# The head mix ahead of the softmax in one float32 matmul, and a new column order for the mixed weights

## The chip, the cores and the metric

The kernel runs on one core of a Trainium2 chip. The metric is the device time of one execution in microseconds, taken over three runs. The core has TensorE (PE, matmuls; PEld is its weight load), VectorE (DVE), ScalarE (ACT), GpSimd (POOL), and SyncE (SP), which issues the transfers.

## The reference

Attention over 2 batches, 12 heads, 448 positions, 64 features a head, in which the heads are mixed before and after the softmax; then two expert layers on the 896 rows of 768 features. All is float32, and the experts' weights come as float64.

```python
scores = scale * np.matmul(q, k.transpose(0, 1, 3, 2))
scores = np.einsum('bhij,hg->bgij', scores, w_pre)
scores = scores - np.max(scores, axis=-1, keepdims=True)
attn = np.exp(scores)
attn = attn / (np.sum(attn, axis=-1, keepdims=True) + 1e-09)
attn = np.einsum('bhij,hg->bgij', attn, w_post)
x = np.matmul(attn, v)          # then heads side by side: 896 x 768
h = x @ w_in                    # first experts: 768 -> 2048 -> 768
x = (h * np.clip(h + 3.0, 0.0, 6.0) / 6.0) @ w_out
h = x @ w_in2                   # second experts
out = (np.maximum(h, 0.0) + alpha * np.minimum(h, 0.0)) @ w_out2
```

## The kernel before

The 448 query rows of a batch are cut into tiles of 120, 120, 120 and 88 rows, eight tiles in all. A tile's scores are made head by head (`qk`): keys and queries are split into two float32r parts (`split_k`, `split_q`), two matmuls give 120 x 448 scores in PSUM, and a copy, mostly on ACT, puts them into S, which holds rows on the partitions and heads side by side.

To mix heads, a matmul needs the heads on the partitions. So a tile is cut into groups of ten rows with all their 12 heads, 120 partitions. Group o of a tile takes the rows o, o + 12, o + 24 and so on (o, o + 8, ... in the tile of 88 rows, whose last 8 rows are a group of their own): 45 groups a batch, 90 in all. `pull` regroups them by a transfer from S. `round_s` rounds the group to float32r (shi, on DVE or, for the first tile, on POOL), and `split_and_norm` takes the remainder (slo, on DVE). `premix` then multiplies by the mixing weights, which lie ten times on the diagonal of a 120 x 120 matrix: high weights times shi, low weights times shi, high weights times slo, three float32r matmuls into one place in PSUM (mx); DVE takes the rows' maximum (nm). `exp` is the softmax's exponential on ACT, with the row sums (sm). One step later `split_and_norm` turns the sums over and multiplies the second mixing matrix by them (wr, on DVE). Three steps later (LAG) `post` mixes with wr, in plain float32, four matmuls with the four key blocks of e as the stationary operand; its result (pt) has keys on the partitions and row x of head g at column 12 x + g. `post_evac` copies it on ACT into MT, where a head's rows lie in their order in the tile: its elements land 12 (or 8) elements and 120 elements apart. `av` multiplies MT by the values for pairs of heads, float32 again, and the result is copied to xT by DVE, or for the last two tiles split at once into two float32r parts by `split_x` (ACT and DVE).

Everything is emitted by hand in one loop over steps, and every engine takes its instructions in that order. Step s issues the regrouping of group s + 4 (PL), then premix(s), the scores due in this step for the next tile (0 to 3 heads), exp(s), the copies of the scores, loads and splits of queries (and, for the first tile of the second batch, of keys), the remainder of group s + 2 with the sums of group s - 1, post(s - 3) with its copy, the value product due for the tile before (every second step or so), and what the experts need early. SP issues all transfers in one queue, in the same order; the regrouping has four buffers, each free again when slo is made. After the loop come the last tile's value products and the experts: products of three float32r matmuls each, with the weights converted beside them by ACT, DVE and POOL.

Of the kernel before, what the change touches and what calls it, by code (L numbers as in the profile page):

```python
# [7 lines left out]
F32 = mybir.dt.float32  # L8
R = mybir.dt.float32r
# [4 lines left out]
ALU = mybir.AluOpType  # L14
# [3 lines left out]
LAG = 3  # steps from a group's premix to its mix after the softmax  # L18
HI = "VVAVVAVVAVVA"  # which engine rounds each head's first keys
PL = 4  # steps from the regrouping of a group's rows to their premix  # L20
EB = 384  # output features of an out-layer that are worked on together
# The high words of 2**-127 and of the largest float32, read as float32.
# [4 lines left out]
def spread(items, lo, hi):  # L27
    """items over the steps lo..hi-1, evenly and in order."""
    out = {}
    n = max(1, hi - lo)  # L30
    for i, it in enumerate(items):
        out.setdefault(lo + i * n // len(items), []).append(it)
    return out
# [3 lines left out]
def kernel(  # L37
    ctx: ExitStack,
    tc: tile.TileContext,
    q: bass.AP,  # [B, 2 D, per query tile: H, rows], the D rows twice  # L40
    k0: bass.AP,  # first batch: [2 D, H / 2, S], the D rows of two heads
    k: bass.AP,  # the others: [B - 1, 2 D, H, S], the D rows twice
    v: bass.AP,  # [B, 112, H, 4, D]: key 112 * t + p at [p, :, t]
    w_pre: bass.AP,  # the 12 x 12 block 10 times on the diagonal
    w_post: bass.AP,
    w_in1: bass.AP,  # int64 words of float64, [block, 128, 768]
# [4 lines left out]
    out: bass.AP,  # transposed  # L51
):
    nc = tc.nc
# [32 lines left out]
    # Pools that end early lie on top of their side, so that what follows lands there.  # L86
# [13 lines left out]
    with tc.manual_schedule():  # L100
# [4 lines left out]
        # ---------------------------------------------------------------- attention  # L105
# [8 lines left out]
        def load_k0(p, z):  # L114
            # the second tile's scores come later to this place
            if p == 0:
                k_st[0] = s_odd.tile([128, H, S], F32, tag="S", name="k0")
            nc.sync.dma_start(out=k_st[0][:, p:z, :], in_=k0[:, p:z, :])
# [17 lines left out]
        # The rows of k and what float32r leaves of them: [hi; lo], or [lo; hi] for the  # L136
        # odd heads of the first batch, which lie on the upper partitions.
# [42 lines left out]
        d_t, hi_t, hl_t, mx_t, e_t, sm_t, wr_t, pt_t = {}, {}, {}, {}, {}, {}, {}, {}  # L180

        def pull(g):
            ti, o, st, xn = groups[g]
            t = late.tile([GP, S], F32, tag="pull", bufs=4, name="pull")
            src = S_t[ti][bass.ds(o, xn, step=st)] if st > 1 else S_t[ti][o:o + xn]
            nc.sync.dma_start(t[:xn * H], src)
            d_t[g] = t

        def round_s(g, eng):
            pn = groups[g][3] * H  # L190
            hi = late.tile([GP, S], R, tag="shi", bufs=3, name="shi")
            eng.tensor_scalar(hi[:pn], d_t[g][:pn], 1.0, 1.0, ALU.mult, ALU.mult)  # L192
            hi_t[g] = hi

        # The rows of group g are split while the row sums of group gn are turned over.
        def split_and_norm(g, gn):
            if gn in sm_t:
                pm = groups[gn][3] * H
                sm = sm_t.pop(gn)[:pm]
                nc.vector.tensor_scalar(sm, sm, 1e-9, None, ALU.add)  # L200
            if g < NG:
                pn = groups[g][3] * H
                if g not in hi_t:
                    round_s(g, nc.vector)
                d, hi = d_t.pop(g)[:pn], hi_t.pop(g)
                lo = late.tile([GP, S], R, tag="slo", bufs=2, name="slo")
                hl_t[g] = (hi, lo)
            if gn in e_t:
                nc.vector.reciprocal(sm, sm)
            if g < NG:  # L210
                nc.vector.tensor_tensor(lo[:pn], d, hi[:pn].bitcast(F32), ALU.subtract)  # L211
            if gn in e_t:
                wr = wr_t[gn] = late.tile([GP, GP], F32, tag="wr", bufs=LAG + 1, name="wr")
                nc.vector.tensor_scalar(wr[:pm, :pm], wpost[:pm, :pm], sm, None, ALU.mult)  # L214

        def premix(g):
            pn = groups[g][3] * H
            hi, lo = hl_t.pop(g)
            m = psA.tile([GP, 512], F32, tag="mx", bufs=2, name="mx")
            nc.tensor.matmul(m[:pn, :S], wph[:pn, :pn], hi[:pn], start=True, stop=False)  # L220
            nc.tensor.matmul(m[:pn, :S], wpl[:pn, :pn], hi[:pn], start=False, stop=False)  # L221
            nc.tensor.matmul(m[:pn, :S], wph[:pn, :pn], lo[:pn], start=False, stop=True)  # L222
            nm = late.tile([GP, 1], F32, tag="nm", name="nm")
            nc.vector.tensor_reduce(nm[:pn], m[:pn, :S], axis=AX.X, op=ALU.max, negate=True)  # L224
            mx_t[g] = (m, nm)
# [11 lines left out]
        def post(g):  # L237
            pn = groups[g][3] * H
            e, wr = e_t.pop(g), wr_t.pop(g)
            p = psA.tile([JP, 512], F32, tag="pt", bufs=2, name="pt")  # L240
            for c in range(NJ):
                nc.tensor.matmul(  # L242
                    p[:, c * pn:(c + 1) * pn], e[:pn, c * JP:(c + 1) * JP], wr[:pn, :pn],
                    start=True, stop=True,
                )
            pt_t[g] = p

        def post_evac(g):
            ti, o, st, xn = groups[g]
            pn = xn * H  # L250
            if ti not in MT:
                MT[ti] = late.tile([JP, NJ, H, GP], F32, tag="MT", bufs=2, name="MT")
            p = pt_t.pop(g)
            dst = MT[ti][:, :, :, o:o + (xn - 1) * st + 1:st].rearrange("p t g x -> p t x g")
            nc.scalar.copy(dst, p[:, :NJ * pn].rearrange("p (t x g) -> p t x g", t=NJ, g=H))  # L255
# [3 lines left out]
        def av(ti, a):  # L259
# [12 lines left out]
            if a % 3 == 2:  # L272
                if ti >= NTILE - 2:
                    for z in range(3):
                        split_x(a - 2 + z, 1, T["i0"], T["i0"] + n, p[:, z, :n], nc.vector)
                else:
                    c0 = T["b"] * S + T["i0"]
                    nc.vector.tensor_copy(xT[:, a - 2:a + 1, c0:c0 + n], p[:, :, :n])

        # which head of which tile is worked on at which step  # L280
# [12 lines left out]
        # ---------------------------------------------------------------- experts  # L293
# [7 lines left out]
        NE = 2  # feature tiles whose results for the first batch have a place of their own  # L301
        NC = 3  # feature tiles whose products for the first batch go ahead
# [16 lines left out]
        # float64 words to float32, rounded to nearest: the exponent's bias changes by  # L319
        # dropping three bits, and the 29 low bits are rounded into the mantissa. What  # L320
        # float32 can't hold becomes zero or its largest number.
# [80 lines left out]
        def split_x(kk, c, a, z, src, eng):  # L402
            if (kk, c) not in x_t:
                x_t[kk, c] = pair(P[f"x{c}"], "x")
            h, l = x_t[kk, c]
            nc.scalar.copy(h[:, a:z], src)
            eng.tensor_tensor(l[:, a:z], src, h[:, a:z].bitcast(F32), ALU.subtract)
# [19 lines left out]
        # An activation in two parts, between which its engines take other work.  # L427
# [54 lines left out]
        # ---------------------------------------------------------------- attention, emitted  # L482
# [8 lines left out]
        for nm, src in (("pre", w_pre), ("post", w_post)):  # L491
            wmix[nm] = (kq if nm == "pre" else late).tile(
                [GP, GP], F32, tag=f"wmix_{nm}", bufs=1, name=f"wmix_{nm}"
            )
# [15 lines left out]
        wpre, wpost = wmix["pre"], wmix["post"]  # L510
        wph = late.tile([GP, GP], R, tag="wph", bufs=1, name="wph")
        wpl = late.tile([GP, GP], R, tag="wpl", bufs=1, name="wpl")
        nc.gpsimd.tensor_scalar(wpre, wpre, scale, 1.0, ALU.mult, ALU.mult)
        nc.gpsimd.tensor_scalar(wph, wpre, 1.0, 1.0, ALU.mult, ALU.mult)
        nc.gpsimd.tensor_tensor(wpl, wpre, wph.bitcast(F32), ALU.subtract)
# [9 lines left out]
        # the experts' first loads and splits, beside the last tile's groups  # L525
# [26 lines left out]
        for s_ in range(-PL, NG + LAG):  # L552
# [36 lines left out]
            if 1 <= s_ + 3 < tiles[1]["s"]:  # L589
                round_s(s_ + 3, nc.gpsimd)  # L590
            if s_ >= -2:
                split_and_norm(s_ + 2, s_ - 1)
# [25 lines left out]
        # ---------------------------------------------------------------- experts, emitted  # L618
# [65 lines left out]
def _laid_out(q, k, v, w_pre, w_post, moe_w_in, moe_w_out, moe2_w_in, moe2_w_out, moe2_alpha):  # L684
    """The inputs' elements in the order in which the kernel reads them."""
# [66 lines left out]
```

## Time and profile before

| | us |
|---|---|
| median of 3 runs | 744.57 |
| lowest, highest | 742.71, 744.76 |
| profiled execution: span from first to last instruction | 740.6 |
| PE busy in it | 707.6 |
| DVE busy | 503.5 |
| ACT busy | 414.9 |
| POOL busy | 345.6 |

The page gives the profiled execution's time as its span; what lies around the span is in the runs' times alone, 4.0 us by the median. The attention takes about the first 273 us of the span, the experts the rest. The busy time of PE is a union of overlapping matmuls, each counted until its last result is out, so it is more than what the matmuls cost one after the other.

### The profile page before, as it was taken

The page shows a single profiled execution, that of the slowest core. Times are in us where ns is not written, and L with a number is a line of the kernel's source. Part 1 is how long each engine was busy: PE and PEld are TensorE (multiplying, and loading weights), DVE is VectorE, ACT ScalarE, POOL GpSimd, SP SyncE. Part 2 cuts the span into 40 slices and gives each one's busy share as a digit, 9 for nine tenths or more (in the row PEclk, how much of TensorE's full clock was granted, in tenths as well). Part 3 has the DMA queues.
Part 4 walks back from the last instruction along what each step waited for, and adds up shares of the span by engine and source line. Part 5 has one row for each costly group of instructions (what it writes and reads, how often), then busy time and mean ns, then how long its engine had stood idle before and what let it go on. Part 6 is the DMA issues. An engine that isn't in the chain of part 4 may idle for free.

```text
span 740.6 us, 11533 instructions
## 1 busy us (share of the span) xinstructions
PE 707.6 (96%) x4254; PEld 627.0 (85%) x4254; DVE 503.5 (68%) x964; ACT 414.9 (56%) x699; POOL 345.6 (47%) x230
## 2 busy tenths in 40 slices
PE   5899978999998999999999999999999999999998
PEld 3678866898876889888889999999999999999997
DVE  7898899888989837777776344346777778435311
ACT  4688866888887745666654354334544444333310
POOL 4341166221315314565657856453555555654530
PEclk9999999999999999999999999999999999999999
DMA  4643454336435202323233432322333332424302
GB/s 150 202 150 111 161 168 96 126 123 215 151 104 101 87 2 92 121 87 127 87 104 128 152 129 90 123 90 82 90 123 101 114 114 103 160 93 161 128 1 74
DMA packets 31621, 85.60 MB, mean 116 GB/s; under 512 B 5198, under 2 KB 21710, under 8 KB 31566
## 3 DMA queue, kind: packets, MB, share of 16 engines
q1 hardware_dynamic: 31566, 84.87, 34.7%
q8 instruction: 34, 0.56, 0.3%
q14 instruction: 21, 0.17, 0.1%
HBM read 62.84 MB, written 2.75 MB: 89 GB/s over the span
## 4 chain that ended last, share of the span: by engine, by line
PE 63%; DVE 18%; issue 9%; POOL 6%; DMA 2%; ACT 2%; SPq 0%; POOLq 0%; DVEq 0%; ACTq 0%
PE p L411 49%; DVE slo L211 5%; PE pt L242 4%; POOL wb L349 4%; PE av L268 4%; DVE nm L224 3%; DVE shi L192 3%; DVE wr L214 2%; PE sc L175 2%; PE mx L220 2%; DMA pull<-S 2%; POOL wlo L360 1%; PE mx L221 1%; PE mx L222 1%; DVE kT L153 1%
## 5 line engine op out<-in xcount | busy, mean ns | idle before, releaser
L360 POOL TENSOR_TENSOR wlo<-wb,whi 128x768 fp32r<-128x768 f32 x64 | 133.0, 2079 | 166.9 <-ACT whi L354 164.4
L349 POOL TENSOR_TENSOR wb<-wb,wst 128x768 int32<-128x768 int32 x64 | 130.5, 2039 | 66.3 <-DVE wb L342 39.4
L411 PE MATMUL p<-xh,wlo 128*128 128x448 f32 x384 | 141.4, 368 | 2.0 <-POOL wlo L360 1.4
L411 PE MATMUL p<-gh,wlo 128*128 128x448 f32 x384 | 141.2, 368 | 0.1
L411 PE MATMUL p<-gh,whi 128*128 128x448 f32 x384 | 141.0, 367 | 0.0
L411 PE MATMUL p<-gl,whi 128*128 128x448 f32 x384 | 141.0, 367 | 0.0
L411 PE MATMUL p<-xh,whi 128*128 128x448 f32 x384 | 140.6, 366 | 0.0
L411 PE MATMUL p<-xl,whi 128*128 128x448 f32 x384 | 140.3, 365 | 0.0
L334 DVE TENSOR_SCALAR wb<-wb 128x768 f32<-128x768 f32 x64 | 64.2, 1003 | 97.0 <-ACT wb L326 96.9
L326 ACT ACTIVATE wb<-wst 128x768 f32<-128x768 f32 x64 | 58.3, 911 | 74.1 <-DMA wst<-in_w_out_dram 43.6
L255 ACT COPY MT<-pt 112x480 f32<-112x480 f32 (+1 forms) x90 | 96.4, 1071 | 1.9 <-PE pt L242 1.9
L242 PEld LDWEIGHTS pt<-wr,e 120*112 120x112 f32 x720 | 85.6, 176 | 9.7 <-ACT MT L255 3.7
L242 PE MATMUL pt<-wr,e 120*112 120x120 f32 x720 | 89.7, 267 | 1.2 <-DVE wr L214 0.7
L232 ACT ACTIVATE e<-mx,nm 120x448 f32<-120x448 f32 (+1 forms) x90 | 57.3, 637 | 49.4 <-DVE sm L200 33.8
L411 PEld LDWEIGHTS p<-xh,wlo 128*128 128x128 f32 x384 | 72.1, 188 | 11.7 <-POOL wlo L360 6.2
L354 ACT CAST whi<-wb 128x768 fp32r<-128x768 f32 x64 | 53.2, 832 | 47.3 <-PE p L411 44.9
L411 PEld LDWEIGHTS p<-gh,wlo 128*128 128x128 f32 x384 | 72.2, 188 | 7.4 <-POOL wlo L360 0.8
L411 PEld LDWEIGHTS p<-gh,whi 128*128 128x128 f32 x384 | 72.2, 188 | 6.5
L411 PEld LDWEIGHTS p<-gl,whi 128*128 128x128 f32 x384 | 72.2, 188 | 6.4
L411 PEld LDWEIGHTS p<-xl,whi 128*128 128x128 f32 x384 | 72.2, 188 | 5.6
L411 PEld LDWEIGHTS p<-xh,whi 128*128 128x128 f32 x384 | 72.1, 188 | 5.6
L175 PE MATMUL sc<-kT,qT 128*120 128x448 f32 (+1 forms) x192 | 58.4, 397 | 15.8 <-DVE kT L153 7.5
(60 smaller groups left out, 1046.5 us busy)
## 6 DMA issues: line engine op xcount, KB each, us to landing
wst<-in_w_in_dram SPq DMA_DIRECT2D x32, 768.0 KB
wst<-in_w_out_dram SPq DMA_DIRECT2D x32, 768.0 KB
pull<-S SPq DMA_DIRECT2D x88, 210.0 KB
qst<-in_q_dram SPq DMA_DIRECT2D x24, 180.0 KB
v<-in_v_dram SPq DMA_DIRECT2D x8, 336.0 KB
kst<-in_k_dram SPq DMA_DIRECT2D x4, 672.0 KB
out_dram<-o SPq DMA_DIRECT2D x12, 224.0 KB
qst<-in_q_dram SPq DMA_DIRECT2D x8, 132.0 KB
```

The lines of the kernel that those rows point to most:

```text
L175: nc.tensor.matmul(p[:n, :S], t[:, o, a:a + n], kT[h], start=(o == 0), stop=(o == 1))
L211: nc.vector.tensor_tensor(lo[:pn], d, hi[:pn].bitcast(F32), ALU.subtract)
L232: nc.scalar.activation(out=e[:pn], in_=m[:pn, :S], func=ACTF.Exp, bias=nm[:pn], accum_out=sm[:pn])
L242: nc.tensor.matmul(p[:, c * pn:(c + 1) * pn], e[:pn, c * JP:(c + 1) * JP], wr[:pn, :pn], start=True, stop=True,)
L255: nc.scalar.copy(dst, p[:, :NJ * pn].rearrange("p (t x g) -> p t x g", t=NJ, g=H))
L268: nc.tensor.matmul(p[64 * o:64 * o + 64, a % 3, :n], v_t[T["b"], h // HC][:, h % HC, c, :], MT[ti][:, c, h, :n], start=(c == 0), stop=(c = ...
L326: nc.scalar.activation(t, s[:, :, 1].bitcast(F32), ACTF.Abs)
L334: nc.vector.tensor_scalar(t, t, W_MAX, W_MIN, ALU.min, ALU.max)
L349: nc.gpsimd.tensor_tensor(n, n, st_t.pop(i)[:, :, 0].bitcast(I32), ALU.add)
L354: nc.scalar.copy(hi, b_t[i])
L360: nc.gpsimd.tensor_tensor(lo, b_t.pop(i), w_t[i][0].bitcast(F32), ALU.subtract)
L411: nc.tensor.matmul(p, wt[a], xt[c], start=(first and z == 0), stop=(last and z == 2))
```

## The change

- `premix` is one float32 matmul on the regrouped rows as they came. `round_s`, the remainder, and the high and low parts of the first mixing matrix are gone.
- The regrouping has PL + 2 = 6 buffers, each free when its premix is done.
- `split_and_norm` becomes `norm`, the turning over of the sums alone.
- The columns of the second mixing matrix are put into another order once, on POOL, so that `post` gives row x of head g at column 10 g + x. `post` always takes all 120 columns.
- MT holds a tile's rows in the order of the groups, so that `post_evac` writes runs of ten elements.
- The rows come back into order behind the value products: `by_row` gives the copy to xT, and the split of the last two tiles, a reading pattern with every tenth row next to each other; a tile of 88 rows is copied in two pieces, 80 and 8 rows.
- Comments are removed, and the first mixing matrix lies in another pool.

```diff
         def pull(g):
-            t = late.tile([GP, S], F32, tag="pull", bufs=4, name="pull")
+            t = late.tile([GP, S], F32, tag="pull", bufs=PL + 2, name="pull")
...
-        def round_s(g, eng):
-            pn = groups[g][3] * H
-            hi = late.tile([GP, S], R, tag="shi", bufs=3, name="shi")
-            eng.tensor_scalar(hi[:pn], d_t[g][:pn], 1.0, 1.0, ALU.mult, ALU.mult)
-            hi_t[g] = hi
...
+        def norm(g):
+            pm = groups[g][3] * H
+            sm = sm_t.pop(g)[:pm]
+            nc.vector.tensor_scalar(sm, sm, 1e-9, None, ALU.add)
+            nc.vector.reciprocal(sm, sm)
+            wr = wr_t[g] = late.tile([GP, GP], F32, tag="wr", bufs=LAG + 1, name="wr")
+            nc.vector.tensor_scalar(wr[:pm], wpost[:pm], sm, None, ALU.mult)
...
         def premix(g):
             pn = groups[g][3] * H
-            hi, lo = hl_t.pop(g)
+            d = d_t.pop(g)
             m = psA.tile([GP, 512], F32, tag="mx", bufs=2, name="mx")
-            nc.tensor.matmul(m[:pn, :S], wph[:pn, :pn], hi[:pn], start=True, stop=False)
-            nc.tensor.matmul(m[:pn, :S], wpl[:pn, :pn], hi[:pn], start=False, stop=False)
-            nc.tensor.matmul(m[:pn, :S], wph[:pn, :pn], lo[:pn], start=False, stop=True)
+            nc.tensor.matmul(m[:pn, :S], wpre[:pn, :pn], d[:pn], start=True, stop=True)
...
-                    p[:, c * pn:(c + 1) * pn], e[:pn, c * JP:(c + 1) * JP], wr[:pn, :pn],
+                    p[:, c * GP:(c + 1) * GP], e[:pn, c * JP:(c + 1) * JP], wr[:pn],
...
-            p = pt_t.pop(g)
-            dst = MT[ti][:, :, :, o:o + (xn - 1) * st + 1:st].rearrange("p t g x -> p t x g")
-            nc.scalar.copy(dst, p[:, :NJ * pn].rearrange("p (t x g) -> p t x g", t=NJ, g=H))
+            p = pt_t.pop(g)[:, :NJ * GP].rearrange("p (t g x) -> p t g x", t=NJ, g=H)
+            r = o * G if st > 1 else o
+            nc.scalar.copy(MT[ti][:, :, :, r:r + xn], p[:, :, :, :xn])
+
+        def by_row(dst, src, n):
+            m = n // G * G
+            d, s = dst[..., :m], src[..., :m]
+            if len(dst.shape) == 3:
+                yield (d.rearrange("p z (x o) -> p z x o", x=G), s.rearrange("p z (o x) -> p z x o", x=G))
+            else:
+                yield (d.rearrange("p (x o) -> p x o", x=G), s.rearrange("p (o x) -> p x o", x=G))
+            if n > m:
+                yield dst[..., m:n], src[..., m:n]
...
-                        split_x(a - 2 + z, 1, T["i0"], T["i0"] + n, p[:, z, :n], nc.vector)
+                        h, l = x_pair(a - 2 + z, 1)
+                        for d, r, s in zip(
+                            (d for d, _ in by_row(h[:, T["i0"]:T["i0"] + n], p[:, z, :n], n)),
+                            (d for d, _ in by_row(l[:, T["i0"]:T["i0"] + n], p[:, z, :n], n)),
+                            (s for _, s in by_row(h[:, T["i0"]:T["i0"] + n], p[:, z, :n], n)),
+                        ):
+                            nc.scalar.copy(d, s)
+                            nc.vector.tensor_tensor(r, s, d.bitcast(F32), ALU.subtract)
                 else:
-                    nc.vector.tensor_copy(xT[:, a - 2:a + 1, c0:c0 + n], p[:, :, :n])
+                    for d, s in by_row(xT[:, a - 2:a + 1, c0:c0 + n], p[:, :, :n], n):
+                        nc.vector.tensor_copy(d, s)
...
+        wpost = late.tile([GP, GP], F32, tag="wpost", bufs=1, name="wpost")
+        nc.gpsimd.tensor_copy(
+            wpost.rearrange("p (g x) -> p x g", g=H), wmix["post"].rearrange("p (x g) -> p x g", g=H)
+        )
...
-        nc.gpsimd.tensor_scalar(wph, wpre, 1.0, 1.0, ALU.mult, ALU.mult)
-        nc.gpsimd.tensor_tensor(wpl, wpre, wph.bitcast(F32), ALU.subtract)
...
-            if 1 <= s_ + 3 < tiles[1]["s"]:
-                round_s(s_ + 3, nc.gpsimd)
-            if s_ >= -2:
-                split_and_norm(s_ + 2, s_ - 1)
+            if s_ - 1 in range(NG):
+                norm(s_ - 1)
```

## Rows read from the trace of the kernel before

**Rows 1.** The page's chain of work that ended last: shares of the span by engine.

```profile
PE 63%; DVE 18%; issue 9%; POOL 6%; DMA 2%; ACT 2%; SPq 0%; POOLq 0%; DVEq 0%; ACTq 0%
```

**Rows 2.** The busy table of five stretches: start and end of the stretch, its length, then for PE, PEld, DVE, ACT and POOL the busy us (and instructions), the granted clock of PE, the share of the transfer engines and their GB/s.

```profile
23.50:58.60 35.10, 30.59 (x190) 23.54 (x191) 31.14 (x85) 27.38 (x58) 14.38 (x21) 1.00 0.56 177
58.60:97.40 38.80, 38.80 (x339) 34.09 (x337) 32.78 (x95) 30.99 (x61) 7.54 (x10) 1.00 0.43 145
97.40:129.70 32.30, 25.24 (x206) 20.46 (x204) 32.30 (x73) 20.98 (x42) 20.88 (x20) 1.00 0.44 119
129.70:175.00 45.30, 45.30 (x409) 40.59 (x408) 39.16 (x118) 38.13 (x76) 10.56 (x13) 1.00 0.41 140
...
221.30:258.00 36.70, 32.20 (x274) 26.99 (x274) 34.25 (x82) 26.68 (x55) 18.00 (x13) 1.00 0.40 96
```

**Rows 3.** The timeline of PE over two steps of a PE-bound stretch: start, length from the first start to the last end, engine, line, operation, tiles, and how many instructions the row merges.

```profile
63.15 0.38 PE L268 MATMUL av<-MT,v 112*64 112x120 f32 x4
63.45 0.47 PE L220 MATMUL mx<-shi,wph 120*120 120x448 f32 x1
63.76 0.37 PE L221 MATMUL mx<-shi,wpl 120*120 120x448 f32 x1
...
64.17 0.57 PE L175 MATMUL sc<-kT,qT 128*120 128x448 f32 x2
64.58 0.98 PE L242 MATMUL pt<-wr,e 120*112 120x120 f32 x8
65.33 0.44 PE L220 MATMUL mx<-shi,wph 120*120 120x448 f32 x1
...
67.34 1.04 PE L268 MATMUL av<-MT,v 112*64 112x120 f32 x16
68.31 0.47 PE L220 MATMUL mx<-shi,wph 120*120 120x448 f32 x1
```

**Rows 4.** PE's instructions grouped by line in three stretches (23.5 to 58.6, 97.4 to 129.7, 221.3 to 258.0): how many, busy us and the mean ns of one, the idle time before them and what ended it. The last row is from PE's waits in 175.0 to 221.3: total us, times, longest.

```profile
L242 PE MATMUL pt<-wr,e 120*112 120x120 f32 x104 | 13.4, 272 | 0.1
L220 PE MATMUL mx<-shi,wph 120*120 120x448 f32 x16 | 7.0, 437 | 3.2 <-POOL shi L192 2.0 <-ACT e L232 0.8 <-POOL qT L161 0.3
L175 PE MATMUL sc<-kT,qT 128*120 128x448 f32 x22 | 6.5, 371 | 0.1
...
L242 PE MATMUL pt<-wr,e 120*112 120x120 f32 x72 | 8.9, 265 | 0.0
L175 PE MATMUL sc<-kT,qT 128*120 128x448 f32 x24 | 7.3, 383 | 7.1 <-ACT S L578 7.0
L268 PE MATMUL av<-MT,v 112*64 112x120 f32 x82 | 5.5, 272 | 0.0
...
L242 PE MATMUL pt<-wr,e 120*112 120x120 f32 x106 | 13.5, 269 | 1.0 <-DVE wr L214 0.7 <-ACT MT L255 0.2
L268 PE MATMUL av<-MT,v 112*64 112x120 f32 x112 | 7.3, 272 | 1.3 <-ACT MT L255 1.3
L220 PE MATMUL mx<-shi,wph 120*120 120x448 f32 (+1 forms) x12 | 5.4, 452 | 0.7 <-DVE sm L209 0.5 <-ACT e L232 0.2
L411 PE MATMUL p<-xh,whi 128*128 128x448 f32 x7 | 2.7, 380 | 0.0
...
PE av L268 <- ACT MT L255: 1.7, 1, 1.7
```

**Rows 5.** Groups of instructions by line and shape, whole run: count, busy us, mean ns of one, idle time before them.

```profile
L192 DVE TENSOR_SCALAR shi<-pull 120x448 fp32r<-120x448 f32 x77 | 39.5, 513 | 0.0
L211 DVE TENSOR_TENSOR slo<-pull,shi 120x448 fp32r<-120x448 f32 x88 | 69.6, 792 | 3.7 <-POOL shi L192 3.6
L255 ACT COPY MT<-pt 112x480 f32<-112x480 f32 x88 | 94.6, 1075 | 1.9 <-PE pt L242 1.9
L255 ACT COPY MT<-pt 112x384 f32<-112x384 f32 x2 | 1.8, 904 | 0.0
L578 ACT COPY S<-sc 120x448 f32<-120x448 f32 x57 | 29.8, 532 | 1.6 <-PE sc L175 1.6
```

**Rows 6.** The page's group of the mix after the softmax, the group of the value products of 88 rows, and the timeline row of the last tile's.

```profile
L242 PE MATMUL pt<-wr,e 120*112 120x120 f32 x720 | 89.7, 267 | 1.2 <-DVE wr L214 0.7
L268 PE MATMUL av<-MT,v 112*64 112x88 f32 x192 | 8.8, 243 | 0.0
268.94 3.86 PE L268 MATMUL av<-MT,v 112*64 112x88 f32 x96
```

**Rows 7.** The busy table of three early stretches, columns as in rows 2.

```profile
24.00:26.00 2.00, 1.62 (x8) 1.30 (x8) 2.00 (x4) 0.10 (x2) 1.31 (x3) 1.00 0.19 73
26.00:32.00 6.00, 5.45 (x33) 4.24 (x31) 5.83 (x18) 4.94 (x12) 1.15 (x2) 1.00 0.87 261
32.00:40.00 8.00, 5.65 (x33) 3.87 (x32) 4.32 (x15) 4.73 (x10) 2.54 (x5) 1.00 0.79 228
```

**Rows 8.** The timeline of ACT behind the last tile's value products, idle time in brackets, and from the waits of 274 to 390 us that of the experts' products for converted weights (total us, times, longest).

```profile
271.02 0.23 ACT L406 CAST xh<-av 128x88 fp32r<-128x88 f32 x1 [0.55 <-PE av L268]
271.57 0.23 ACT L406 CAST xh<-av 128x88 fp32r<-128x88 f32 x1 [0.32 <-DVE xl L407]
274.07 0.91 ACT L326 ACTIVATE wb<-wst 128x768 f32<-128x768 f32 x1
...
PEld p L411 <- POOL wlo L360: 6.6, 12, 1.8
```

## What I predicted

> **What bounds the kernel now.** I read the chain of the whole run first: 63% of it is TensorE (PE) and 18% VectorE (DVE) [rows 1]. So both matter, and the next question is where each does. The busy table by stretch answers it [rows 2]: look for stretches in which one engine has no idle time. From 58.6 to 97.4 us and from 129.7 to 175.0 PE is busy for the whole stretch. From 97.4 to 129.7 it is DVE that is busy for all 32.30 us while PE has 25.24. In 23.5 to 58.6 and 221.3 to 258.0 DVE is near full too. So the attention alternates: PE-bound stretches pay for every PE nanosecond that is added, and DVE-bound stretches pay back what DVE loses. The granted clock is 1.00, its 2.4 GHz level, in all of them.
>
> Busy time of a pipelined matmul is not its price; its price is the distance between starts. In a PE-bound step [rows 3] the premix's second pass starts at 63.76 and what follows the third at 64.17: 0.203 us each, so 0.61 for three. The 8 passes of the mix after the softmax take 0.98 with a last one of 0.265 long, so (0.98 - 0.265) / 7 = 0.102 each, 0.82 for eight. A step without the value product runs from 63.45 to 65.33, 1.88 us; one with it from 65.33 to 68.31, 2.98. The value product therefore costs 1.10.
>
> From these prices and the counts of three slow stretches [rows 4] comes the idle time that PE could get rid of:
> - 23.5 to 58.6 (the first value product ends it): 16 x 0.61 + 22 x 0.203 + 13 x 0.82 + 1 x 1.10 = 26.0 of 35.1; idle 9.1.
> - 97.4 to 129.7 (72 / 8 = 9 whole steps): 9 x 0.61 + 24 x 0.203 + 9 x 0.82 + 5 x 1.10 = 23.2 of 32.3; idle 9.1.
> - 221.3 to 258.0: 12 x 0.61 + 13.2 x 0.82 + 7 x 1.10 + 20 x 0.203 (first expert products; one of three like rows is shown) = 29.9 of 36.7; idle 6.8.
> In 175.0 to 221.3 one wait on the copy of the mixed weights counts, 1.7 [rows 4].
>
> **The change, part by part.**
>
> **DVE loses the rounding and the remainder.** Per group shi (0.513) and slo (0.792) go: 39.5 + 69.6 = 109 us of DVE, and 11 roundings of GpSimd (POOL) [rows 5]. In 97.4 to 129.7 that leaves DVE about 32.3 - 9 x 1.3 to 32.3 - 9 x 1.84 (there slo is dearer), 16 to 21 us for work that PE needs 23 for; DVE is no longer the bound. Nothing that is left of DVE's work stands in front of the premix: its input is the regrouping transfer itself, issued four steps ahead.
>
> **PE: one float32 matmul instead of three float32r ones.** The trace has no float32 matmul of 448 columns, but it has two kinds of narrow ones. The mix after the softmax shows two passes for each (720 for 90 x 4). The value products show what a column costs: 96 passes of 88 columns in 3.86 us [rows 6] are (3.86 - 0.243) / 95 = 0.0381 each, 16 of 120 columns in 1.04 [rows 3] are (1.04 - 0.266) / 15 = 0.0516. They run in pairs, one on each half of the output: four take 0.38, which is 0.266 and one distance of 0.10, not three of 0.0516 [rows 3]. So a pair, and each pass in it, is 0.076 and 0.103: 0.84 ns for each column, and next to nothing fixed. One pass of 448 columns is then 448 x 0.84 = 0.376, two are 0.752, against 0.61: +0.143 for a group, +12.9 us for 90, where PE is the bound. Bounds: if the halves of a pair were really served in turn, a column costs half and a pass no less than the 0.203 of a float32r pass of that width: 0.406, a gain of 0.203 a group (18.3 us). From above four float32r passes: 0.812, +0.203 (18.3 us). I take 0.752, since the four in 0.38 speak for passes side by side.
>
> The Trainium skill ("FP8 and Floating Point Precision", TensorE Precision Notes) says that true float32 takes four passes through the array. The trace shows two instructions for each; at 0.84 ns for a column each is worth two. By four passes at float32r's price the premix would cost the upper bound, and the sum below would lose its gain almost wholly.
>
> **Regrouping transfers.** Six buffers instead of four, freed by the premix and no longer by slo. It matters in the beginning only: from 24 to 26 us the transfers run at 73 GB/s for want of a buffer, then at 261 and 228 [rows 7]. All of 24 to 40 at 261 would be (146 + 1566 + 1824) / 261 = 13.5 us instead of 16: the first nine groups come at most 2.5 us sooner, whatever DVE does. So of the 9.1 us of the first stretch I keep 3.0.
>
> **The copy of the mixed weights (ACT).** 480 scattered elements take 1.075, 384 take 0.904: 1.78 ns each over a fixed 0.22. A dense copy of 448 takes 0.532, so (0.532 - 0.22) / 448 = 0.70 [rows 5]; runs of ten should come near 0.22 + 480 x 0.70 = 0.56; the bounds are 0.56 and 1.075. 90 x 0.5 = 46 us of ACT go, but ACT is the bound in no stretch [rows 2]: worth the 1.7 us wait above and a part of 0.8 in the first stretch. Without that cover the copy is what the value product waits for.
>
> **The turned column order** (the permuted weights once on POOL, which is busy 14.4 of 35.1 us in the first stretch [rows 2], and 120 instead of 96 columns for two groups) is nothing. The rows come back into order when the value product leaves PSUM. On DVE, which has room now, that costs nothing; for the last tile it does. Its six copies and six subtractions alternate, ACT then DVE, 0.55 a pair, and the next conversion follows at 274.07 directly [rows 8]. 88 rows become a piece of 80 and one of 8: at about 0.53 and 0.38 a pair of pieces, 0.36 more for each of six, 2.2 in all on that thread. The experts then wait for converted weights (6.6 us in 12 waits [rows 8]), so a later start of the conversions is not swallowed; but PE itself starts on the first pieces at once. I take 1.5, bounds 0 and 2.5.
>
> The Trainium skill ("Advanced Engine Details and Errata", PSUM Cachelines) has 8-byte lines in PSUM and asks for two elements in a row; the reading by every tenth element breaks that. By the scattered price of 1.78 ns against 0.70, 80 elements would take 0.09 longer in each of 12 instructions, 1.0 us more at the end; the trace has no such read.
>
> **The sum.** Idle time that goes: 6.1 in the first stretch; 7.1 in the second (POOL has 20.9 us of work there [rows 2] and would fill 24 to nine tenths, so I keep 2); 1.7; 5.8 in the last (I keep 1). Together 20.7. Against it +12.9 on PE and +1.5 at the end: -6.3. The profile's span is 740.6, the median 744.6, 4 us around the span that the change doesn't touch. 744.6 - 6.3 = 738.3.
>
> **The rivals.**
> 1. *The slow stretches stay slow because DVE only stood in the way of others* (slower). In 97.4 to 129.7 POOL's remainders of the keys and queries, in the beginning the transfers, set the pace: then only 1.7 + 5.8 and 3.3 of the first stretch go, 10.8, against 14.4: 748.2. It decides below 14.4 us of recovered idle time, 54% of the 26.7. For it: POOL's 20.9 us there and 261 GB/s early. Against: PE's step would still be longer than POOL's share. 16%.
> 2. *Four full passes.* +18.3 + 1.5 against 20.7: 743.7, no change. For it: nothing in the trace shows a wide float32 pass. Against: the slope of the value products. 12%.
> 3. *A float32 pass costs one column slot.* -18.3: 20.7 + 18.3 - 1.5 = 37.5 faster, 707. Against: a pair of 120 columns takes 0.103. 4%.
> 4. *The copy is as slow as before*: ACT is hidden anyway; the forecast loses 1.7 to 2.5 and stays faster. It is inside the range.
>
> **How the numbers follow.** Forecast 68%: 738.3, its own range 732 (all 26.7 go and the end costs nothing: 744.6 - 13.8 = 730.8) to 743 (15.7 go, 2.5 at the end). Taking in most of rivals 1 and 2, the range is 731.5 to 747.5. 0.3% is 2.2 us, about what the measurement can tell from no change. Faster: 0.68 x 0.94 + 0.04 + 0.12 x 0.25 = 0.71. Slower: 0.16 x 0.75 + 0.12 x 0.25 = 0.15. Same: 0.14.
>
> **What would show it.** Right: two premix passes 0.37 to 0.38 apart; steps of about 2.02 and 3.12 in the PE-bound stretches; no stretch with DVE full; the stretch of the second batch's keys down from 32.3 to some 27; the copy near 0.6. Wrong: passes 0.2 or 0.4 with a gap; PE idle on POOL's keys around 100 to 120 us; the first expert products later than the attention's end by more than 2 us.

## The result, and the profile after

The changed kernel takes 733.25 us (median of 4 runs, 732.57 to 733.72) against 744.66 (742.71 to 745.42): 0.984 of the time before, 95% interval 0.982 to 0.986, 11.4 us less. All these are times of undisturbed executions; of the runs below only e12 had others, 788.6 and 2483.5 us.

Of the 11.4 us the profiled spans show 8.7 (740.6 to 731.9). The changed kernel's profiled execution took 733.72 us, 1.8 more than its span, and in the 43 executions of the kernel before that were taken beside the experiments, 1.7 to 1.9 us lie around the span as well. So it is 1.8 and not the 4.0 that I read from the median: the profiled execution of the kernel before took about 742.4, 2.3 less than its median, and the one of the changed kernel 0.5 more than its own. The other 2.7 of the 11.4 us are this difference between executions and have no place in the two traces. A part of it may go with the clock: of those 43 executions the 17 with a mean granted clock of 0.993 or less took 745.4 in the median and the four at 1.00 took 743.5, and the profiled one is at 1.00.

The busy table of the changed kernel, in stretches that begin and end with the premix of a group: 0 to 16, 16 to 31, 31 to 41, 41 to 60, 60 to 77, 77 to 89, and from there to the end of the attention. Columns as in [rows 2]:

```profile
22.73:54.68 31.95, 29.32 (x176) 21.48 (x175) 18.50 (x61) 22.72 (x58) 7.39 (x11) 1.00 0.67 207
54.68:92.68 38.00, 38.00 (x294) 28.93 (x293) 19.42 (x61) 23.09 (x58) 4.95 (x8) 1.00 0.44 140
92.68:120.64 27.96, 27.96 (x225) 21.57 (x223) 23.26 (x56) 18.55 (x47) 21.07 (x22) 1.00 0.52 143
120.64:168.73 48.09, 48.09 (x390) 37.36 (x389) 23.55 (x82) 29.57 (x74) 9.89 (x14) 1.00 0.43 142
168.73:212.82 44.09, 44.09 (x350) 33.55 (x348) 26.40 (x79) 32.82 (x78) 7.11 (x8) 1.00 0.46 145
212.82:242.91 30.09, 30.09 (x249) 23.22 (x248) 20.40 (x54) 20.60 (x51) 15.38 (x12) 1.00 0.47 117
242.91:261.15 18.24, 18.24 (x203) 16.00 (x201) 5.74 (x18) 8.07 (x22) 2.97 (x4) 1.00 0.01 2
```

PE has no idle time from 54.7 us to the end of the attention; DVE is full nowhere. Where DVE was full for 32.3 us [rows 2] it is busy for 23.3 of 28.0, and PE, which had 25.2 of 32.3, is the bound. The chain of work that ended last, on the changed kernel's page, says the same (shares of the span):

```profile
PE 81%; issue 8%; POOL 6%; DMA 2%; DVE 1%; ACT 1%; SPq 0%; POOLq 0%; DVEq 0%; ACTq 0%
```

DVE's share of the chain went from 18% [rows 1] to 1%, PE's from 63% to 81%. The next table gives the us between the starts of the premixes in both timelines, with what the prediction's terms give for each stretch:

| stretch | before | after | difference | forecast |
|---|---|---|---|---|
| start to group 0 | 23.5 | 22.7 | -0.8 | |
| groups 0 to 16 | 35.1 | 32.0 | -3.1 | -3.8 with the start |
| 16 to 31 | 35.8 | 38.0 | +2.2 | +2.1 |
| 31 to 41 | 35.3 | 28.0 | -7.3 | -5.7 |
| 41 to 60 | 45.3 | 48.1 | +2.8 | +2.7 |
| 60 to 77 | 44.8 | 44.1 | -0.7 | +0.7 |
| 77 to 89 | 34.4 | 30.1 | -4.3 | -4.1 |
| 89 to the end of the last value product | 18.6 | 18.3 | -0.3 | |
| from there to the end | 467.8 | 470.7 | +2.9 | +1.5 with the row above |

From group 16 on, traces of like kernels agree to 0.1 us in such a stretch (e11, the changed kernel once more, has 38.0, 28.0, 48.1, 44.1 and 30.1). Up to group 16 they don't: the changed kernel takes 54.7 us to there, e11 55.3, and e4, which differs in the last tile alone, 53.8.

The price of the premix, on PE's timeline in a PE-bound stretch (start, us, engine, line, operation, count):

```profile
59.80 1.01 PE L202 MATMUL mx<-pull,wmix_pre 120*120 120x448 f32 x2
61.06 0.98 PE L222 MATMUL pt<-wr,e 120*112 120x120 f32 x8
61.88 0.92 PE L202 MATMUL mx<-pull,wmix_pre 120*120 120x448 f32 x2
62.29 0.92 PE L175 MATMUL sc<-kT,qT 128*120 128x448 f32 x2
63.05 0.98 PE L222 MATMUL pt<-wr,e 120*112 120x120 f32 x8
63.97 1.04 PE L259 MATMUL av<-MT,v 112*64 112x120 f32 x16
64.94 0.64 PE L202 MATMUL mx<-pull,wmix_pre 120*120 120x448 f32 x1
```

A pair of steps, one of them with a value product, goes from 59.80 to 64.94: 5.14 us, where it took 4.86 [rows 3]. That is 0.14 for each premix. Inside a step the premix and two score passes take 63.05 - 61.88 = 1.17; without 2 x 0.203 for the scores, 0.76 for the two passes.

### The profile page after: what moved, and what is told of

It is laid out like the page before. It is cut to its first block, busy times and chain, and to the rows that moved or that the text cites. A ratio compares the mean times of both kernels' runs of the same rounds, so it can differ in the third digit from the quotient of the medians.

```text
span 731.9 us, 11176 instructions
## 1 busy us (share of the span) xinstructions
PE 714.7 (98%) x4164; PEld 612.5 (84%) x4164; DVE 425.2 (58%) x803; ACT 379.0 (52%) x705; POOL 328.7 (45%) x218
## 4 chain that ended last, share of the span: by engine, by line
PE 81%; issue 8%; POOL 6%; DMA 2%; DVE 1%; ACT 1%; SPq 0%; POOLq 0%; DVEq 0%; ACTq 0%
PE p L413 50%; PE mx L202 10%; PE pt L222 10%; PE av L259 6%; PE sc L175 5%; POOL wb L348 4%; POOL wlo L359 2%; DMA pull<-S 1%; DMA qst<-in_q_dram 1%; DVE wb L333 0%; ACT wb L325 0%; POOL qT L162 0%; DVE xl L273 0%; ACT xh L272 0%; SPq L118 0%
## 5 line engine op out<-in xcount | busy, mean ns | idle before, releaser
L359 POOL TENSOR_TENSOR wlo<-wb,whi 128x768 fp32r<-128x768 f32 x64 | 131.3, 2051 | 166.6 <-ACT whi L353 166.6
L413 PE MATMUL p<-xh,whi 128*128 128x448 f32 x384 | 142.9, 372 | 0.0
L204 DVE TENSOR_REDUCE nm<-mx 120x1 f32<-120x448 f32 (+1 forms) x90 | 56.1, 623 | 74.0 <-PE mx L202 73.9
L175 PE MATMUL sc<-kT,qT 128*120 128x448 f32 (+1 forms) x192 | 81.5, 524 | 8.3 <-DVE kT L153 7.6
L202 PE MATMUL mx<-pull,wmix_pre 120*120 120x448 f32 x180 | 86.7, 564 | 2.6 <-DMA pull<-S 1.5
```

The costliest lines, as they stand in the source:

```text
L175: nc.tensor.matmul(p[:n, :S], t[:, o, a:a + n], kT[h], start=(o == 0), stop=(o == 1))
L202: nc.tensor.matmul(m[:pn, :S], wpre[:pn, :pn], d[:pn], start=True, stop=True)
L359: nc.gpsimd.tensor_tensor(lo, b_t.pop(i), w_t[i][0].bitcast(F32), ALU.subtract)
L413: nc.tensor.matmul(p, wt[a], xt[c], start=(first and z == 0), stop=(last and z == 2))
```

## The experiments

Each kernel is compared with the kernel before on its own chip (medians 744.6 to 745.0 on the three chips). e2, e5, e6, e7, e8 and e10 get the second mixing matrix already turned from outside, so the one copy of it on POOL, 0.56 us at the start, is missing there.

**The two halves apart: e1 and e2.** e1 is the changed kernel with the old column order, e2 the kernel before with the new one. The edit of e1, against the changed kernel (e2 makes the reverse one in the kernel before):

```diff
-                    p[:, c * GP:(c + 1) * GP], e[:pn, c * JP:(c + 1) * JP], wr[:pn],
+                    p[:, c * pn:(c + 1) * pn], e[:pn, c * JP:(c + 1) * JP], wr[:pn, :pn],
...
-            nc.scalar.copy(MT[ti][:, :, :, r:r + xn], p[:, :, :, :xn])
+            dst = MT[ti][:, :, :, o:o + (xn - 1) * st + 1:st].rearrange("p t g x -> p t x g")
+            nc.scalar.copy(dst, p[:, :NJ * pn].rearrange("p (t x g) -> p t x g", t=NJ, g=H))
...
+        wpost = wmix["post"]
```

> The float32 premix on unsplit rows with its six buffers, and the old column order with its scattered copy (1.075 us) and its plain last split. If DVE's relief and PE's price are what the change is about: some 732.5 us (730.5 to 735.5), the change's 733.3 less 2.5 that the split of the last tile in pieces costs, and up to 2 for value products that wait for the slower copy. If the faster copy on ACT carried a good part of the gain: 737 or more.

> The kernel before with the new column order alone (the weights come turned from outside, which saves a tile). If ACT is hidden: 744.7 (743 to 747), 1.7 to 2.5 us of waits for the copy gone and some 2.6 more behind the last tile. If the copy counts: 740 or less.

e1 takes 732.2, 0.982 (0.979 to 0.986) of before: the whole gain. Its copy is as slow as before, and still PE waits for no copy of the mixed weights; its groups 60 to 77 take 44.0 us, where the prediction took the 1.7 us of that wait to go by the faster copy. e2 takes 743.2, 0.9974 (0.9957 to 0.9991): within what was expected, a gain near what can be told from none. On top of the premix the new order is worth nothing that these runs can tell (733.25 with it, 732.2 without), although it works as written. ACT's copies of the mixed weights, grouped by line, in the changed kernel, then in e1:

```profile
L235 ACT COPY MT<-pt 112x480 f32<-112x480 f32 x88 | 50.7, 576 | 3.0 <-PE pt L222 3.0
```

```profile
L236 ACT COPY MT<-pt 112x480 f32<-112x480 f32 (+1 forms) x90 | 94.7, 1052 | 2.4 <-PE pt L222 2.4
```

44 us of ACT lie between the two, and the time is the same: ACT was hidden, and stays so.

**PE's price and DVE's relief apart: e6 and e5.** e6 puts three float32r passes back, on the unsplit rows, so DVE keeps its relief; the product of the remainder is left out. e5 keeps the float32 premix and gives DVE its old load, whose result nobody reads:

Against the changed kernel, first e6, then e5:

```diff
-            nc.tensor.matmul(m[:pn, :S], wpre[:pn, :pn], d[:pn], start=True, stop=True)
+            nc.tensor.matmul(m[:pn, :S], wph[:pn, :pn], d[:pn].bitcast(R), start=True, stop=False)
+            nc.tensor.matmul(m[:pn, :S], wpl[:pn, :pn], d[:pn].bitcast(R), start=False, stop=False)
+            nc.tensor.matmul(m[:pn, :S], wpl[:pn, :pn], d[:pn].bitcast(R), start=False, stop=True)
```

```diff
+            if s_ >= -2 and s_ + 2 < NG:
+                dead_split(s_ + 2)
```

> The changed kernel with three float32r passes on the unsplit rows in place of the float32 matmul; the remainder's pass takes the rows again, so its product is left out. PE's price alone: if PE is the bound of the whole attention now and a group pays 0.143, 90 groups give back 12.9: 720.5 (718 to 725). If another engine took over where DVE left off: 728 or more.

> The changed kernel, and beside it DVE still rounds each group and takes its remainder, into a tile that nobody reads. If the gain is DVE's relief: 749 (746 to 754), as the slow stretches come back with all of their idle time while the PE-bound ones keep the 0.146 us a group. If it came from the buffers or the copy: 733 to 736.

e6 takes 723.3, 0.970 (0.967 to 0.974) of before: 21.4 us less, and 10.0 less than the changed kernel. Groups 41 to 60 take 45.3 us as in the kernel before, 16 to 31 take 35.8, 77 to 89 28.3. The busy table of e6 over groups 41 to 60 (nearly) has PE busy for the whole time and DVE for half of it:

```profile
119.20:164.50 45.30, 45.30 (x409) 40.63 (x408) 23.96 (x83) 30.23 (x76) 9.87 (x14) 1.00 0.47 156
```

So the change is a relief of some 21 us, bought with 10 us of PE. The whole price of 12.9 isn't paid, because groups 31 to 41 (27.4 against 28.0) and 0 to 16 (31.6 against 32.0) give back only 0.6 and 0.4 of the 1.4 and 2.3 that their passes cost. In the first PE stands idle for 0.3 us alone (27.04 busy of 27.37), so no wait is the cause, and it stays open; the second varies by more than 0.4 from trace to trace, and there the regrouping transfers are what PE waits for:

```profile
PE mx L202 <- DMA pull<-S: 3.2, 2, 2.3
```

(e6's waits of PE up to 252 us: total, times, longest.)

e5 takes 757.2, 1.016 (1.013 to 1.019): the slow stretches are back, and more than that, while groups 16 to 31 and 41 to 60 keep the changed kernel's 38.0 and 48.1 us. Its busy table in two of the slow ones:

```profile
100.00:135.00 35.00, 28.18 (x205) 20.54 (x202) 33.62 (x75) 16.87 (x42) 20.46 (x20) 0.95 0.40 111
...
232.00:269.00 37.00, 32.01 (x241) 23.16 (x239) 33.51 (x75) 20.63 (x51) 15.90 (x12) 0.95 0.37 95
```

DVE is nearly full again, and PE idle for 5 to 7 us; so it was DVE's two instructions that held the attention up, not something that the change removed beside them. Nobody waits for their result in e5: what counts is the time that they take on DVE, not the longer way of the rows to the premix. The 757 lie 3 above what I gave as the upper end: I had let the slow stretches come back at their old length, but groups 31 to 41 take 37.5 against 35.3, 60 to 77 47.3 against 44.8, 77 to 89 38.1 against 34.4. The granted clock of 0.95, where the kernel before has 1.00 [rows 2], is a part of it: by these two rows an estimate is (1 - 0.95) x 28.18 = 1.4 and (1 - 0.95) x 32.01 = 1.6 us. In groups 60 to 77 the clock is 1.00 and explains nothing. What 11 more roundings on DVE add was not measured.

**The buffers: e3, e9, e12.** I had said that six buffers instead of four matter in the beginning only.

All three against the changed kernel. e3:

```diff
-            t = late.tile([GP, S], F32, tag="pull", bufs=PL + 2, name="pull")
+            t = late.tile([GP, S], F32, tag="pull", bufs=4, name="pull")
```

e9 has this too, and the second batch's values, in the order of the step, ahead of pull(g) instead of behind it:

```diff
+            for ti in range(tps, NTILE, tps):
+                if s_ == tiles[ti]["s"] + tiles[ti]["ng"] + LAG:
+                    for c in range(4):
+                        load_v(tiles[ti]["b"], c)
```

e12 is e9 with these loads one step sooner:

```diff
+                if s_ == tiles[ti]["s"] + tiles[ti]["ng"] + LAG - 1:
```

> The changed kernel with four buffers for the regrouped rows instead of six. If the buffers matter only in the beginning, where the transfers are the bound: 734.5 (733.5 to 736). If they matter in all steps: 738 or more; if not at all: 733.2.

e3 takes 741.4, 0.9952 (0.9937 to 0.9967): 8 us of the 11 are gone (7 against e11, on the same chip), and my expectation was wrong. "738 or more" is met, but not for the reason beside it: groups 16 to 31, 31 to 41, 41 to 60 and 77 to 89 take what they take with six buffers, to 0.1 us, so it isn't all steps. 7.3 of them are lost in one place, groups 60 to 77 (51.4 us against 44.1). e3's timeline of PE there, and then of SP's queue (start, us, engine, line, operation, idle time before it in brackets):

```profile
172.16 0.98 PE L222 MATMUL pt<-wr,e 120*112 120x120 f32 x8
177.48 1.87 PE L259 MATMUL av<-MT,v 112*64 112x120 f32 x16 [4.34 <-DMA v<-in_v_dram]
...
181.67 1.80 PE L222 MATMUL pt<-wr,e 120*112 120x120 f32 x8
```

```profile
171.94 0.81 SPq L186 DMA_DIRECT2D pull<-S  x1
172.80 1.89 SPq L122 DMA_DIRECT2D v<-in_v_dram  x4
```

The second batch's values are issued in the very step whose value product needs them, behind that step's regrouping in the one queue of SP. With four buffers, freed by the premix, the regrouping waits for the premix of its own step (170.99 to 171.91), and the values wait behind it. Ahead of the value product PE stands idle for 4.34 us. That is not the whole of the 7.3: the mix behind it takes 1.80 instead of 0.98, and e3's busy table shows a lower granted clock there (columns as in [rows 2]):

```profile
176.00:182.00 6.00, 4.52 (x22) 3.28 (x23) 0.80 (x3) 0.12 (x1) 0.00 (x0) 0.57 0.58 145
182.00:188.00 6.00, 6.00 (x43) 4.80 (x42) 3.79 (x10) 3.21 (x8) 1.38 (x1) 0.86 0.28 96
```

By these two rows the clock took an estimated (1 - 0.57) x 4.52 + (1 - 0.86) x 6.00 = 2.8 us of PE's busy time; with the 4.3 of waiting that is 7.1 of the 7.3. In the changed kernel the same loads go out two steps sooner, at 165.61, for a value product at 170.81 (the changed kernel's timelines of SP's queue and of PE):

```profile
164.75 0.81 SPq L186 DMA_DIRECT2D pull<-S  x1
165.61 1.89 SPq L122 DMA_DIRECT2D v<-in_v_dram  x4
```

```profile
170.81 1.04 PE L259 MATMUL av<-MT,v 112*64 112x120 f32 x16
```

> The changed kernel with four buffers, as e3, but in the step that loads the second batch's values these loads are issued ahead of the step's regrouping. If what four buffers cost is that the regrouping holds the transfer queue while the values wait behind it (4.3 us of waiting, and matmuls at the 1.2 GHz level for some us behind it): 734.5 (733 to 736), e3's 741.4 less 7.3. If four buffers hold up every step: 740 or more.

e9 takes 740.0, 0.992 (0.989 to 0.995), with executions from 735.7 to 742.0. Groups 60 to 77 take 49.0: one regrouping, that of the step before, still stood in front of the loads, and PE still waited for 3.2 us, with a granted clock of 0.87 and 0.84 in the six microseconds around the wait and the six behind it. The gain is less than expected, and by its time alone e9 would fit the rival (740 or more); but its other stretches, too, are those of the changed kernel to 0.1 us from group 16 on.

> e9 with the values' loads one step sooner still, ahead of the regrouping of the step before. In e9 one regrouping that waits for a buffer still stood in front of them and PE waited 3.2 us. If the queue is what four buffers cost: no such wait, no matmuls at 1.2 GHz, the stretch of groups 60 to 77 back to 44.6 us, and the whole at 734.5 (733 to 736). If four buffers cost more than that: 738 or more.

e12 takes 735.9, 0.987 (0.984 to 0.991): with four buffers, and only the loads moved past the second waiting regrouping, 5.5 of e3's 8 us are back. The profiled execution is the one of 2483.5 us, so the stretches can't be read from it; that the clock and the wait are gone is inferred from the time. What is left, some 2 us, would fit the beginning: with four buffers group 16 starts at 55.0 to 57.8 us (e3, e7, e8, e9, e10), with six at 53.8 to 55.3 (the changed kernel, e4, e11), 1.9 sooner in the mean. The two ranges overlap, so this isn't shown.

**The last tile's split: e4.**

```diff
+            if ti == NTILE - 1:
+                nc.scalar.copy(MT[ti][:, :, :, o:o + (xn - 1) * st + 1:st], p[:, :, :, :xn])
+                return
...
+                if ti == NTILE - 1:
+                    for z in range(3):
+                        split_x(a - 2 + z, 1, T["i0"], T["i0"] + n, p[:, z, :n], nc.vector)
```

> The changed kernel, but the last tile's mixed weights are written in row order as before (nine scattered copies), so that its split needs no pieces. If the pieces delay the experts' conversions and that is never made up: 731 (730 to 732). If the delay is swallowed: 733.2.

e4 takes 732.1, 0.983 (0.981 to 0.984), against 0.984 (0.982 to 0.986) with the pieces: in these times not to be told from nothing. On one chip, e4 takes 2.2 less than e11, and e8 2.4 less than e7, from which it differs in this alone. The traces tell more. The timeline of ACT in the changed kernel, behind the last value products, ends with:

```profile
263.77 0.23 ACT L272 CAST xh<-av 128x80 fp32r<-128x80 f32 x1 [0.23 <-DVE xl L273]
264.30 0.17 ACT L272 CAST xh<-av 128x8 fp32r<-128x8 f32 x1 [0.31 <-DVE xl L273]
264.37 0.91 ACT L325 ACTIVATE wb<-wst 128x768 f32<-128x768 f32 x1
```

The first conversion starts at 264.37, 3.2 us after the end of the last value product (261.22); before it was 1.3 after it, at 274.07 [rows 8], and in e4 it is 1.3 again. From that end to the end of the span it takes 469.6 to 471.3 us in the eight traces with pieces (the changed kernel 470.7, e2, e3, e5, e6, e7, e9, e11), and 467.8 to 468.9 in the five without (before, e1, e4, e8, e10). So the pieces cost between 0.7 and 3.5 us by the traces and some 2 by the times, with my 1.5 near.

**Both prices where they are cheap: e7, e8, e10.** If PE's price is lost in PE-bound stretches and DVE's load costs nothing there, each group should go the way that its stretch has room for.

```diff
+        SPLIT = [*range(16, 31), *range(41, 62)]
...
+            if g in hl_t:
+                hi, lo = hl_t.pop(g)
+                nc.tensor.matmul(m[:pn, :S], wph[:pn, :pn], hi, start=True, stop=False)
+                nc.tensor.matmul(m[:pn, :S], wpl[:pn, :pn], hi, start=False, stop=False)
+                nc.tensor.matmul(m[:pn, :S], wph[:pn, :pn], lo, start=False, stop=True)
+            else:
+                d = d_t.pop(g)
+                nc.tensor.matmul(m[:pn, :S], wpre[:pn, :pn], d[:pn], start=True, stop=True)
```

e7 and e8 (with e4's last tile) have four buffers beside the split rows, and so the queue of e3; e10 is e8 with the values' loads ahead of their step's regrouping.

> The changed kernel with four buffers; groups 16 to 30 and 41 to 61, which PE bounds, go through three float32r passes on split rows, the others through the float32 matmul. If a group pays 0.146 on PE where PE is the bound and DVE has room there: 36 x 0.146 = 5.3 less, with 1 more for the buffers 729 (727 to 732). If DVE's load brings the waits back: 733 or more.

> The same with the last tile in row order: both gains add up, 727 (725 to 730). If they don't: as the better of the two alone, 729 to 731.

> e8 with the same move. If its stretch from 165 to 213 us (46.4 against 44.6 with six buffers) is the same queue: 727.5 (726 to 729.5). If not: as e8, 730.

> The changed kernel once more, beside these on one chip: 733.3 (732 to 735).

e7 takes 732.6, 0.984 (0.982 to 0.985), 3.6 above what I expected; e8 730.2, 0.982 (0.980 to 0.985), just above its range and within that of the case that the gains don't add up. Groups 16 to 31 and 41 to 60 are as cheap as they should be, 35.8 and 45.3 us as in the kernel before. But the value loads are late again: groups 60 to 77 take 45.2 us in e7 and 47.4 in e8, against 43.9 in e10. In e7's trace 3.2 us more than in the changed kernel's lie before group 16, where like kernels differ too. With the loads moved, e10 takes 728.8, 0.978 (0.975 to 0.981), and the changed kernel, run beside it as e11, 734.3, 0.986 (0.983 to 0.988). The intervals don't meet: 5.5 us better than the change, 16 better than before. Some 2 of the 5.5 are e4's last tile; against e4 e10 is 3.3 us better.

## Why the prediction was right

**The price of the premix** (0.752 from the slope of the narrow value products): 0.76 in the step, +0.147 a group in groups 16 to 31 and +0.146 in 41 to 60, where +0.143 was forecast. The second rival, 0.812, would have cost 0.20 a group; the third, 0.406, would have given as much back; both are out by the same rows. The rule of the Trainium skill ("FP8 and Floating Point Precision", TensorE Precision Notes), four passes for true float32, fits the 0.76 us if a pass takes one cycle of the 2.4 GHz level for each column, 4 x 448 / 2.4 = 0.747 us by estimate; at the 0.203 of a float32r pass it doesn't.

**That DVE was what held the slow stretches up** (e5), and that POOL's work on the keys would not take its place (the first rival): POOL has 21.07 us of work in groups 31 to 41, as before, and PE no idle time beside it. The 2 us that I kept for it there were too many: -7.3 instead of -5.7. How DVE holds PE up, the prediction does not say, and the rows name another engine: PE waits there for ACT's copies of the scores, 7.0 us [rows 4]. These copies stand behind the exponential in ACT's order, and the exponential waits for the maximum (nm) that DVE makes. ACT's group of it in the kernel before, from 97.4 to 129.7 us:

```profile
L232 ACT ACTIVATE e<-mx,nm 120x448 f32<-120x448 f32 x10 | 6.3, 635 | 12.4 <-DVE nm L224 11.1 <-DVE sm L200 1.4
```

e5 against the changed kernel shows the same by DVE's load alone: over groups 31 to 41 ACT waits for nm for 9.1 us in the changed kernel and 20.9 in e5, and PE for the copies of the scores not at all and 6.8 us.

**The beginning**: -3.9 with the start, -3.8 forecast. That it comes so near is partly luck, as e11 gives -3.3 there and e4 -4.8. The forecast let DVE's relief take 6.1 of the 9.1 idle us and kept 3.0 for the transfers; the changed kernel keeps 2.6 (29.32 busy of 31.95). From 24 to 26 us the transfers now run at 233 GB/s instead of 73 [rows 7]. The busy table of the changed kernel there:

```profile
24.00:26.00 2.00, 2.00 (x8) 0.98 (x6) 1.32 (x5) 1.57 (x4) 0.00 (x0) 1.00 0.84 233
```

But the gain is not in that rate: e5, with DVE's old load, has 259 GB/s there and starts group 16 at 59.4 us, 0.8 later than the kernel before. Nor does the rate need six buffers: e3 with four has 196.

**The size** was short: 11.4 us, not 6.3. The table shows 1.6 of the difference in groups 31 to 41 and 1.4 in 60 to 77, the end 1.1 dearer; 2.7 are the difference between the executions. e6 puts it another way: the relief with the dearer end was 21.4 where I had 19.2, and the price 10.0 where I had charged all 90 groups with 12.9, though in the first groups the transfers, by my own reckoning, would hide it. The bounds beside the forecast were also added up wrongly: the terms named there give 730.8 and 744.3, not 732 and 743.

**The step that was wrong**: "It matters in the beginning only", of the buffers. I had not asked what is queued behind the regrouping. The change frees a buffer at the premix, two steps later than slo did; with four buffers the value loads in SP's queue come two steps later than with six, and e3 is 8 us slower for it. So the two more buffers keep the change from losing most of its gain; whether they would bring the kernel before a gain of their own, no run shows. **The credit for the copy** was misplaced too: the 1.7 us of waiting for it are gone in e1, which has the slow copy.

**The new read order** cost nothing where it was read. ACT's conversions of the last two tiles, first in the kernel before, where neighbours are read, then in the changed kernel, where each reads every tenth element:

```profile
L406 ACT CAST xh<-av 128x120 fp32r<-128x120 f32 x6 | 1.6, 268 | 3.1 <-PE av L268 1.7 <-DVE xl L407 1.4
L406 ACT CAST xh<-av 128x88 fp32r<-128x88 f32 x6 | 1.4, 233 | 2.3 <-DVE xl L407 1.3 <-PE av L268 1.0
...
L272 ACT CAST xh<-av 128x120 fp32r<-128x120 f32 x6 | 1.6, 258 | 4.0 <-PE av L259 2.6 <-DVE xl L273 1.4
L272 ACT CAST xh<-av 128x80 fp32r<-128x80 f32 x6 | 1.4, 226 | 1.8 <-DVE xl L273 0.9 <-PE av L259 0.9
```

120 such elements take 258 ns, where 120 neighbours took 268, and 80 take 226, where 88 neighbours took 233. DVE's copies of 360 go from 526 to 530 ns. The rule of the Trainium skill ("Advanced Engine Details and Errata", PSUM Cachelines), two elements in a row, isn't borne out by these reads; whether it holds for matmuls, which the page names, no run here shows. What costs at the end is the number of pieces: 1.9 us until the first conversion, 2.2 forecast.

## What to carry to other kernels

Work out the relief and the price stretch by stretch: the same edit gave 7.3 us in one stretch and took 2.8 in another, and a kernel that picks the way by stretch (e10) beats both. When a trace names an engine that a wait ended on, ask what that engine had waited for before: here PE waited for ACT, and ACT for DVE. When a buffer is held longer, ask what stands behind the instruction that waits for it in its queue, not only whether its own data are late. A faster copy on an engine that is hidden is worth what its waits were worth, here nothing.

## What the runs showed of the hardware

An idle time of 4.3 us on PE (e3) cost an estimated 2.8 more behind it: the granted clock was 0.57 in the six microseconds around the end of the wait and 0.86 in the next six, eight passes took 1.80 us instead of 0.98, the 1.2 GHz level, and only then came 1.00 again. Two float32 passes of 448 columns take 0.76 us, three float32r passes 0.61. ACT's conversion of 120 elements from PSUM takes 258 ns when its source steps by ten elements and 268 when it is dense; ACT's copy of 480 takes 1.05 us with a scattered target (e1) and 0.58 with runs of ten (the changed kernel).
